# Sliding-window attention and an MLP mixer on one core: transpositions as units of their own, a planner with other constants, and new orders

## The chip, the cores and the metric

The kernel runs on one core of a Trainium2 chip. Five engines take part. TensorE (PE in the profile; PEld are its weight loads) multiplies matrices into PSUM, VectorE (DVE), ScalarE (ACT) and GpSimd (POOL) read PSUM or SBUF and write SBUF, and SyncE (SP) only issues DMAs. GpSimd issues DMAs too: all loads that change the type from float32 to bfloat16 go through its queue. The metric is the device time of one execution in microseconds (us). Three executions of the kernel before took 195.54, 192.81 and 198.23 us, so its median is 195.54 us.

## The reference

Four batches, eight heads, 768 positions, 64 channels a head. A query sees the last 128 positions and the first four (the sinks). The mixer follows, over positions (w_tok1, w_tok2) and then over channels (w_ch1, w_ch2).

```python
scores = scale * np.matmul(q, k.transpose(0, 1, 3, 2))
keep = is_sink | in_window                    # first 4 keys, or the last 128
scores = np.where(keep, scores, -1000000000.0)
a = np.exp(scores - np.max(scores, axis=-1, keepdims=True))
a = a / (np.sum(a, axis=-1, keepdims=True) + 1e-09)
x = np.matmul(a, v)                           # then heads side by side: (4, 768, 512)
...
xt = x.transpose(0, 2, 1)
h = np.maximum(xt @ w_tok1, 0.0) @ w_tok2
u = x + h.transpose(0, 2, 1)
h2 = np.maximum(u @ w_ch1, 0.0) @ w_ch2
return (u + h2).astype(np.float32)
```

## The kernel before, in words

Attention goes by 16 **pairs**: pair p holds two heads of batch p // 4. Pairs 0 to 3 load q and k as float32 on SyncE's queue and cast them on an engine; pairs 4 to 15 load them as bfloat16 on GpSimd's queue (`load_q_or_k`, L1398), one DMA each for pairs 4 to 7 and two halves each from pair 8 on. v goes to six buffers on GpSimd's queue (`load_v`, L177; pair p uses buffer p % 6), with a column of ones that sums the softmax's denominators.

q and k have to stand with the channels on the partitions. For pairs 0 to 7 TensorE transposes them into PSUM (`turn`, L586, or `transposed`, L604), and ScalarE or VectorE copies them to SBUF (`prepare`, L514). From pair 8 on (`BY_DMA`) SyncE issues DMA transposes from SBUF to SBUF (L542). There are three buffers for the transposed k (`kTb`, L214: kT0, kT1, kT2; pair p uses kT of p % 3). After the transposition the sinks' columns of kT are copied to a tile kTs (L196, by GpSimd or VectorE, and by ScalarE for the early pairs).

Then come, for each pair: scores in three groups (`scores`, L640), for pairs 0 to 3 with the mask added by a matmul ahead of them (`masked`), an exp on ScalarE into pT (L680), for later pairs a mask applied to pT by VectorE (L699) or GpSimd (L691), the sinks' scores for two pairs at a time (`score_sinks`, L718), and pT times v (`pv`, L745), whose result VectorE divides by the sum of the weights (L766, L769) into x_sb.

The mixer over positions is `mix_h` (L870, with w_tok1) and `mix_u` (L902, with w_tok2). Its result u is transposed by TensorE in the first batches and by DMA in the later ones (L931). The mixer over channels is `mix_channels`: a first stage with w_ch1 (`v1`, or seven products of sums in place of eight products in `by_seven`, L1108, with the differences of L1094) and a second stage with w_ch2 that always goes by seven products of sums (`products`, L1250; the sums of w_ch2 are made by L1471, those of v1 by L1216; VectorE adds the products up in o_sb, L1262; SyncE or ScalarE stores o_sb, L1272).

**What sets the order.** TensorE's work is cut into units, in named streams: s scores, m masks, t transpositions and o pT times v of pairs 0 to 3; g and h the mixer over positions of batch 0; a the scores of pairs 4 to 15, called bursts, two groups each (`burst`, L469); v pT times v and k the mixer over positions of the later pairs and batches; c the first stage over channels; x and y the second stage (x of two row tiles, y of one). The string `ORDERED` says in which order units are issued on TensorE: "k4 y0 a9" is unit 4 of stream k, unit 0 of y, unit 9 of a. The string `LOADS` is the order of GpSimd's loads after the first ones: q5, k5 and v5 belong to pair 5, t1 and t2 are the two w_tok, c0 to c3 the parts of w_ch1, d0 to d3 those of w_ch2. Everything else (which engine copies what, when, which PSUM bank a unit gets, where on each queue a DMA stands) is chosen while the program is built, by a planner (`Plan`, from L320): it keeps a clock for each engine with assumed costs and issues whatever can begin first by that clock (`other`, L383; `commit_pe`, L405; `run`, L425). A load is taken to be finished `RECEIPT` ns after the queue's assumed time, and no more than `LANES` loads may be under way. On the chip each engine then runs its instructions strictly in the order written, with waits on semaphores.

In the kernel before, the transpositions of q and k of pair p + 1, for pairs 5 to 7, are a piece (`transposed`) of the burst that holds the first scores of pair p. So bursts a2, a3 and a5 start with 48 small transposing matmuls (units a0 and a1 are pair 4's transpositions).

## Time and profile before

| | |
|---|---|
| median of three executions | 195.54 us (192.81 to 198.23) |
| the profiled execution | 194.1 us, span of its instructions 192.1 us |
| TensorE busy | 180.8 us (94%), 2270 matmuls recorded of 2273 |
| VectorE, ScalarE, GpSimd busy | 161.1, 109.1, 81.9 us |
| granted TensorE clock | 1.00 |
| software DMA queue (GpSimd's loads) | 11.80 MB, 56864 packets |
| hardware DMA queue (SyncE's and ScalarE's) | 13.64 MB, 25136 packets |

The 2.0 us between the span and the execution's own time are around the program: before its first and after its last instruction. TensorE is the engine with the most work. An idle stretch of TensorE before the last matmul lengthens the run unless a later wait becomes shorter by it; idle time elsewhere counts only if TensorE comes to wait for it.

### The profile page before, as it was taken

How to read it: one execution, taken by the hardware profiler on the slowest of the kernel's cores; microseconds unless marked ns; L12 is line 12 of the kernel's file. 1: busy time of each engine (PE TensorE's matmuls, PEld its weight loads, DVE VectorE, ACT ScalarE, POOL GpSimd, SP SyncE). 2: the span in 40 equal slices, each digit the busy share in tenths (PEclk: the TensorE clock that was granted, in tenths of full speed). 3: DMA queues.
4: the chain of work that ended last, by engine and by line, in shares of the span. 5: the costliest groups of instructions: out<-in, count | busy, mean ns of one | idle time of the engine just before them, and what ended most of it. 6: DMA issues, size and time to landing. Idle time of an engine off the chain costs nothing.

```text
span 192.1 us, 5590 instructions
## 1 busy us (share of the span) xinstructions
PE 180.8 (94%) x2270; PEld 132.9 (69%) x2273; DVE 161.1 (84%) x340; ACT 109.1 (57%) x205; POOL 81.9 (43%) x132
## 2 busy tenths in 40 slices
PE   6688979799999999999999999999999999999992
PEld 1345667467667778885776789876777887667881
DVE  4466667697999799999999999989999986699953
ACT  4698858998896551528955760767453111773000
POOL 7198856497865398994262493040000000000000
PEclk9999999999999999999999999999999999999999
DMA  5999999999999999999999996250211204400144
GB/s 177 252 309 193 187 197 194 178 179 173 152 167 151 122 116 144 167 143 281 158 147 125 151 116 136 109 218 3 58 29 27 55 3 164 164 3 0 55 138 139
DMA packets 82601, 26.32 MB, mean 137 GB/s; under 512 B 70032, under 2 KB 80272, under 8 KB 82576
## 3 DMA queue, kind: packets, MB, share of 16 engines
q0 software_dynamic: 56864, 11.80, 77.6%
q1 hardware_dynamic: 25136, 13.64, 36.3%
q10 hardware_dynamic: 576, 0.52, 0.8%
q8 instruction: 18, 0.29, 0.6%
q14 instruction: 7, 0.06, 0.1%
HBM read 26.75 MB, written 6.29 MB: 172 GB/s over the span
## 4 chain that ended last, share of the span: by engine, by line
PE 60%; DMA 30%; DVE 3%; POOL 2%; issue 2%; SPq 0%
PE ps L187 60%; DMA w_ch<-in_moe_w_ch_dram 19%; DMA q_f<-in_q_dram 7%; DMA w_tok<-in_moe_w_tok_dram 4%; DVE q_f L1471 1%; DVE v_sums L1216 1%; POOL k_bf L172 1%; DVE o_sb L1262 1%; POOL v_aug L180 1%; DVE pT L699 1%; POOL w_ch L205 1%; SPq L135 0%; POOL q_bf L196 0%; PE ps L584 0%
## 5 line engine op out<-in xcount | busy, mean ns | idle before, releaser
L680 ACT ACTIVATE pT<-ps 128x1024 bf16<-128x1024 f32 (+1 forms) x48 | 44.0, 956 | 13.7 <-PE ps L187 13.6
L194 ACT ACTIVATE parts<-ps 128x384 f32<-128x384 f32 x54 | 24.4, 493 | 26.7 <-PE ps L187 22.5
L187 PE MATMUL ps<-uT,w_ch 128*128 128x384 bf16 x168 | 34.0, 326 | 0.1
L187 PEld LDWEIGHTS <-v1T 128*128 128x128 bf16 x288 | 27.8, 98 | 5.9 <-DVE q_f L1471 0.5
L1150 DVE CUSTOM_DVE_ANT_0 v1T<-ps,parts 128x384 bf16<-128x384 f32 x54 | 28.6, 552 | 3.4 <-PE ps L187 2.5
L187 PEld LDWEIGHTS <-w_ch 128*128 128x128 bf16 x204 | 19.3, 98 | 11.0 <-issue 0.6
L200 ACT ACTIVATE v1T<-ps 128x384 bf16<-128x384 f32 x39 | 18.9, 495 | 8.6 <-PE ps L187 8.0
L187 PEld LDWEIGHTS <-v_sums 128*128 128x128 bf16 x216 | 20.8, 98 | 3.0 <-issue 0.6
L187 PE MATMUL ps<-uT_sums,k_f 128*128 128x384 bf16 x108 | 22.6, 326 | 0.0
L187 PEld LDWEIGHTS <-w_tok 128*128 128x128 bf16 x192 | 18.4, 98 | 4.4 <-issue 0.5
L691 POOL TENSOR_SCALAR_AFFINE_SELECT pT<-pT 128x256 bf16<-128x256 bf16 (+1 forms) x28 | 15.0, 569 | 13.4 <-issue 9.3
L180 POOL DMA_DIRECT2D v_aug<-in_v_dram x16 | 17.0, 1063 | 7.0 <-PE ps L187 3.6
L187 PE MATMUL ps<-q_f,v1T 128*128 128x256 bf16 x144 | 19.2, 273 | 0.3 <-DVE q_f L1471 0.2
L187 PEld LDWEIGHTS <-k_f 128*128 128x128 bf16 x144 | 13.7, 98 | 7.7
L187 PE MATMUL ps<-w_ch,v1T 128*128 128x256 bf16 x144 | 19.0, 273 | 0.0
L187 PE MATMUL ps<-v_aug,pT 128*128 128x65 bf16 x352 | 18.0, 194 | 1.0 <-DMA v_aug<-in_v_dram 1.0
L1262 DVE TENSOR_TENSOR o_sb<-ps,u_sb 128x512 f32<-128x512 f32 (+1 forms) x32 | 17.1, 548 | 1.9 <-PE ps L187 1.9
L187 PEld LDWEIGHTS <-pT 128*128 128x128 bf16 x352 | 16.1, 98 | 3.2 <-DMA v_aug<-in_v_dram 1.3
L187 PE MATMUL ps<-q_f,v_sums 128*128 128x256 bf16 x144 | 18.2, 273 | 0.2 <-DVE o_sb L1262 0.2
L769 DVE TENSOR_TENSOR x_sb<-ps,recip 128x384 bf16<-128x384 f32 x32 | 17.3, 552 | 0.6
L1262 DVE TENSOR_TENSOR o_sb<-ps,o_sb 128x256 f32<-128x256 f32 (+1 forms) x24 | 12.9, 551 | 3.4 <-PE ps L187 3.2
L172 POOL DMA_DIRECT2D k_bf<-in_k_dram x16 | 13.4, 840 | 5.0 <-DMA q_bf<-in_q_dram 2.7
(88 smaller groups left out, 293.3 us busy)
## 6 DMA issues: line engine op xcount, KB each, us to landing
v_aug<-in_v_dram POOLq DMA_DIRECT2D x16, 192.0 KB, 11.0
w_ch<-in_moe_w_ch_dram POOLq DMA_DIRECT2D x8, 384.0 KB, 10.0
out_dram<-o_sb SPq DMA_DIRECT2D x6, 512.0 KB, 2.8
out_dram<-o_sb SPq DMA_DIRECT2D x10, 256.0 KB, 2.8
q_f<-in_q_dram SPq DMA_DIRECT2D x4, 384.0 KB, 6.5
k_f<-in_k_dram SPq DMA_DIRECT2D x4, 384.0 KB, 6.8
q_bf<-in_q_dram POOLq DMA_DIRECT2D x16, 96.0 KB, 8.3
k_bf<-in_k_dram POOLq DMA_DIRECT2D x16, 96.0 KB, 10.7
```

What stands on the lines that cost most here:

```text
L172: in_order(nc.gpsimd.dma_start(out=out[:, h], in_=rows[:, h]))
L180: in_order(nc.gpsimd.dma_start(out=v_aug.rearrange("p i t d -> p (i t) d")[:, :, 0:D], in_=v[b].rearrange("h s d -> (h s) d")[2 * hp * S:2 ...
L187: issue(nc.tensor.matmul(*args, skip_group_check=True, **kwargs))
L194: in_order(nc.scalar.activation(out, in_, AF.Copy))
L200: in_order(nc.scalar.activation(out, in_, AF.Relu))
L205: return in_order(nc.gpsimd.dma_start(out=out, in_=in_))
L680: in_order(nc.scalar.activation(part(tiles["pT", p][:, :, ds(2 * g, 2)]), of_keys(tiles["ps_s", p, g])[:, :, 0:width(g)], AF.Exp, scale=scale,
L691: in_order(nc.gpsimd.affine_select(out=pt, in_=pt, compare_op=ALU.is_ge, fill=0.0, base=-n, pattern=[[0, nk], [1 - 2 * n, P]], channel_mul ...
L699: in_order(nc.vector.tensor_tensor(out=pt, in0=pt, in1=m, op=ALU.min))
L769: in_order(nc.vector.tensor_tensor(out=x_sb[b][:, ts(half, QH), ts(hp, 2 * D)].rearrange("p t (i d) -> p t i d", i=2), in0=tiles["ps_o", p ...
L1150: in_order(nc.vector._custom_dve(TENSOR_ADD_SAT, out=v1_of(i, half), in0=ps, in1=kept[:, n], s0=HUGE, s1=0.0,))
L1262: in_order(nc.vector.tensor_tensor(out=sb(*out), in0=tiles["ps_out", b, t0, key[0]], in1=in1(), op=ALU.add,))
```

## The change

Four edits, all of them in how the program is ordered; the arithmetic and the number of matmuls stay as they are.

1. The transpositions of q and k for pairs 5, 6 and 7 leave the bursts. Each becomes a unit of its own (one burst with the single piece `transposed`), in a new stream w: w0 and w1 are pair 4's q and k (a0 and a1 before), w2, w3 and w4 are pairs 5, 6 and 7. Stream a has 18 units in place of 20, all numbers two lower.
2. The planner takes a load to finish 600 ns later (`RECEIPT` 1500 to 2100) and allows seven loads under way where it allowed eight.
3. The planner lets two readers of one PSUM bank on different engines follow each other, the second 60 ns after the first has ended, where before it let them run side by side.
4. `ORDERED` and `LOADS` are new strings.

All lines below the string stand one line further down after the change, and those below the planner's class ten.

```diff
     ORDERED = (
-        "t0-1 m0-1 s0-1 t2 m2 s2 t3 m3 s3 o0 m4 s4 t4 m5 o1 s5 t5 o2 m6 s6 t6 m7 s7 t7 o3 m8 s8 o4 a0 s9-10 m9 "
...
+        "t0-1 m0 s0 m1 t2 s1 m2 t3 s2 m3 o0 s3 t4 m4 o1 s4 o2 t5 m5 s5 t6 m6 s6 w0 t7 m7 s7 m8 o3 s8 o4 s9 w1 "
...
     LOADS = (
-        "q4 v1 t1 k4 v2 t2 v3 k5 q5 k6 q6 c0 v4 c3 c2 v5 q7 v6 k7 q9 c1 k9 q8 d3 k8 d1 v7 v11 d0 k10 d2 v8 "
...
+        "q4 v1 k5 k4 t1 q5 v2 q6 t2 v3 k6 v4 v5 c1 d2 k7 q7 c2 q8 c3 c0 v6 v7 d0 k8 k9 d1 q9 k11 d3 k13 q11 "
+        "v8 q10 v9 v10 k10 q12 v11 k12 q13 q14 k14 k15 v12 q15 v13 v14 v15 "
     )
...
-    LATER = "cxyakv"
+    LATER = "cxyakvw"
...
-    LANES = 8
+    LANES = 7
...
-    RECEIPT = 1500.0
+    RECEIPT = 2100.0
...
+            self.reads = []
...
-                e = min(op.cost, key=lambda e: max(self.free[e], r) + op.cost[e] + BIAS * (e == "DVE"))
-                t = max(self.free[e], r)
+                at = {
+                    e: max([self.free[e], r] + [x[1] for x in op.reads if x[0] != e]) for e in op.cost
+                }
+                e = min(op.cost, key=lambda e: at[e] + op.cost[e] + BIAS * (e == "DVE"))
+                t = at[e]
...
+                    last = [None, 0.0]
+                    for r in readers:
+                        r.reads.append(last)
...
+                    for x in op.reads:
+                        x[:] = [o[2], self.free[o[2]] + 60.0]
...
         prepare(first)
-        units += [turn(first, n) for n in range(2)]
+        turned = [turn(first, n) for n in range(2)]
...
             if p + 1 < min(BY_DMA, last + 1):
-                with_first.append(transposed(p + 1))
+                turned.append(burst(transposed(p + 1)))
...
-        return units, tokens, out
+        return units, tokens, out, turned
...
-    streams.update(zip("akv", attention_and_tokens()))
+    streams.update(zip("akvw", attention_and_tokens()))
```

What the strings and the planner make of this is shown at three places.

GpSimd's instructions from the cast of v's sinks on, before: v_aug1, v_aug2 and v_aug3 are v of pairs 1 to 3, k_bf_287 is k of pair 4, the casts are q and k of pair 3.

```order
L196 CAST v_sink_143<-uT_sums_145 128x520
L180 DMA v_aug1_96<-in_v_dram 128x12x64
L205 DMA w_tok1_164<-in_moe_w_tok1_dram 128x6x256
L167 DMA k_bf_287<-in_k_dram 128x2x384
L180 DMA v_aug2_97<-in_v_dram 128x12x64
L196 CAST q_bf_345<-q_f_159 128x2x6x64
L205 DMA w_tok2_165<-in_moe_w_tok2_dram 128x2x768
L196 CAST k_bf_390<-k_f_161 128x2x6x64
L180 DMA v_aug3_98<-in_v_dram 128x12x64
```

The same place after the change: k_bf_272 and q_bf_325 are pair 5, k_bf_286 is pair 4, q_bf_436 is pair 6.

```order
L197 CAST v_sink_143<-uT_sums_145 128x520
L181 DMA v_aug1_96<-in_v_dram 128x12x64
L168 DMA k_bf_272<-in_k_dram 128x2x384
L168 DMA k_bf_286<-in_k_dram 128x2x384
L206 DMA w_tok1_164<-in_moe_w_tok1_dram 128x6x256
L168 DMA q_bf_325<-in_q_dram 128x2x384
L197 CAST q_bf_358<-q_f_159 128x2x6x64
L197 CAST k_bf_370<-k_f_161 128x2x6x64
L181 DMA v_aug2_97<-in_v_dram 128x12x64
L168 DMA q_bf_436<-in_q_dram 128x2x384
L206 DMA w_tok2_165<-in_moe_w_tok2_dram 128x2x768
L181 DMA v_aug3_98<-in_v_dram 128x12x64
```

v of pair 2 now stands behind both casts, w_tok2 behind three more loads of q and k, and w_tok2 is no longer between the two casts.

GpSimd's instructions around the loads of v of pair 8 (v_aug2_97) and of k of pair 10 (k_bf_1160), before. kT2 and kT0 are the transposed k of pairs 8 and 9; copying their sinks' columns waits for the DMA transposes.

```order
L172 DMA k_bf_1160<-in_k_dram 128x6x64 x2
L205 DMA w_ch2_167<-in_moe_w_ch2_dram 128x3x512
L180 DMA v_aug2_97<-in_v_dram 128x12x64
L691 AFFINE_SELECT pT_1127<-pT_1127 128x2x128 x2
L691 AFFINE_SELECT pT_1127<-pT_1127 128x128 x2
L172 DMA k_bf_1248<-in_k_dram 128x6x64 x2
L180 DMA v_aug4_99<-in_v_dram 128x12x64
L196 COPY kTs_142<-kT2_111 64x4 x2
L180 DMA v_aug3_98<-in_v_dram 128x12x64
```

The same place after the change: v of pair 8 is v_aug2_97 as before, k of pair 10 is k_bf_1560, k_bf_1348 is pair 13, q_bf_1381 pair 11 and q_bf_1456 pair 10.

```order
L206 DMA w_ch2_167<-in_moe_w_ch2_dram 128x3x512
L197 COPY kTs_142<-kT2_111 64x4 x2
L173 DMA k_bf_1348<-in_k_dram 128x6x64 x2
L173 DMA q_bf_1381<-in_q_dram 128x6x64 x2
L197 COPY kTs_142<-kT0_109 64x4 x2
L181 DMA v_aug2_97<-in_v_dram 128x12x64
L173 DMA q_bf_1456<-in_q_dram 128x6x64 x2
L701 AFFINE_SELECT pT_1445<-pT_1445 128x2x128 x4
L181 DMA v_aug3_98<-in_v_dram 128x12x64
L181 DMA v_aug4_99<-in_v_dram 128x12x64
L173 DMA k_bf_1560<-in_k_dram 128x6x64 x2
```

Both loads stood ahead of the two copies of the sinks' columns; now both stand behind them, k of pair 10 behind a masking of four instructions and two loads of v as well, and the last part of w_ch2 is issued ahead of them all.

VectorE's last instructions before, o_sb0 being the sums of two row tiles (unit stream x) and o_sb2 those of one (stream y):

```order
L1262 TENSOR_TENSOR o_sb0_3128<-ps_94,o_sb0_3128 128x2x256 x2
L1262 TENSOR_TENSOR o_sb2_3180<-ps_94,u_sb_2609 128x256
L1262 TENSOR_TENSOR o_sb2_3180<-ps_94,o_sb2_3180 128x256
L1262 TENSOR_TENSOR o_sb0_3128<-ps_94,u_sb_2609 128x2x256
L1262 TENSOR_TENSOR o_sb2_3180<-ps_94,u_sb_2609 128x256
L1262 TENSOR_TENSOR o_sb2_3180<-ps_94,o_sb2_3180 128x256
```

And after:

```order
L1272 TENSOR_TENSOR o_sb0_3129<-ps_94,o_sb0_3129 128x2x256
L1272 TENSOR_TENSOR o_sb2_3167<-ps_94,o_sb2_3167 128x256 x2
L1272 TENSOR_TENSOR o_sb0_3129<-ps_94,u_sb_2599 128x2x256
L1272 TENSOR_TENSOR o_sb2_3167<-ps_94,u_sb_2599 128x256
L1272 TENSOR_TENSOR o_sb0_3129<-ps_94,o_sb0_3129 128x2x256
```

The last sum of the program is now one of two row tiles (512 elements a partition, stored by SyncE) where it was one of one row tile (256 elements, stored by ScalarE).

1 line of the change is left out of this document (removed), and 25 rows, old and new, of the table ORDERED.

## The prediction

> **What bounds the kernel now.** I start with the busy times of the page and then the table of stages (busy microseconds in each stretch, then the granted clock, the DMA share and GB/s).
>
> ```profile
> PE 180.8 (94%) x2270; PEld 132.9 (69%) x2273; DVE 161.1 (84%) x340; ACT 109.1 (57%) x205; POOL 81.9 (43%) x132
> 0.00:8.00 8.00, 5.42 (x43) 2.00 (x43) 3.56 (x19) 4.22 (x7) 4.03 (x11) 1.00 0.81 207
> 8.00:16.00 8.00, 6.22 (x110) 3.50 (x114) 5.75 (x14) 7.24 (x14) 5.67 (x7) 1.00 1.44 278
> 16.00:24.00 8.00, 7.67 (x160) 5.00 (x162) 4.61 (x14) 7.06 (x12) 7.44 (x10) 1.00 1.67 187
> 24.00:40.00 16.00, 13.53 (x267) 9.89 (x267) 11.38 (x28) 13.11 (x27) 9.53 (x14) 1.00 1.67 188
> 40.00:72.00 32.00, 31.65 (x475) 22.96 (x464) 28.90 (x58) 23.92 (x46) 23.44 (x36) 1.00 1.93 150
> 72.00:128.00 56.00, 55.84 (x740) 43.35 (x738) 53.91 (x112) 31.45 (x54) 30.35 (x56) 1.00 1.56 154
> 128.00:184.00 56.00, 56.00 (x463) 42.42 (x461) 49.39 (x94) 22.08 (x49) 1.49 (x3) 1.00 0.20 59
> 184.00:192.00 8.00, 4.51 (x42) 3.79 (x39) 3.63 (x7) 0.00 (x0) 0.00 (x0) 1.00 0.47 154
> ```
>
> TensorE (the first busy figure) sets the time. It lacks 7.2 us of the first 40 (2.6 + 1.8 + 0.3 + 2.5), 0.5 us of the next 88 and nothing from 128 to 184 us; 3.5 us go behind its last matmul. So an order can win at most some 5 us, nearly all of it before 40 us. The same figures say what it can lose: from 40 us on no transfer is late now, and whatever becomes late there is paid in full.
>
> Next come TensorE's own rows in order of time; in brackets is its idle time and what ended it.
>
> ```profile
> 15.93 0.35 PE L158 MATMUL ps<-ident,q_bf 64*128 64x64 bf16 x12
> 26.08 0.36 PE L187 MATMUL ps<-v_aug,pT 128*128 128x65 bf16 x6 [1.00 <-DMA v_aug<-in_v_dram]
> 33.37 0.38 PE L187 MATMUL ps<-qT,kT 64*64 64x256 bf16 x8 [0.23 <-ACT pT L680]
> 35.46 0.40 PE L190 MATMUL ps<-ident,u_sb 128*128 128x128 bf16 x4 [0.84 <-ACT qT L194]
> 36.18 0.83 PE L190 MATMUL ps<-ident,u_sb 128*128 128x128 bf16 x12 [0.32 <-DVE u_sb L919]
> ...
> 67.51 0.83 PE L187 MATMUL ps<-q_f,v1T 128*128 128x256 bf16 x6 [0.22 <-DVE q_f L1471]
> 73.10 1.47 PE L187 MATMUL ps<-q_f,v_sums 128*128 128x256 bf16 x12 [0.16 <-DVE o_sb L1262]
> 75.50 0.35 PE L187 MATMUL ps<-v_aug,pT 128*128 128x65 bf16 x6
> 87.18 0.54 PE L187 MATMUL ps<-qT,kT 64*64 64x256 bf16 x16
> ```
>
> The last two have no bracket: v of pair 8 (75.50) and the transposed q and k of pair 10 (87.18) are there when TensorE comes.
>
> **The change, part by part.** The sum is made against the profiled execution, 194.1 us.
>
> *Switches of form.* TensorE's array changes between 128x128, 64x128, 64x64 and 64x32. Counted in the order, such changes go from 68 to 79: a transposition that left its burst needs its own switch, and so do score bursts now cut up by other units.
>
> ```profile
> 18.08 0.48 PE L187 MATMUL ps<-mask_add,ident 128*128 128x384 bf16 x2
> 18.50 0.34 PE L187 MATMUL ps<-qT,kT 64*128 64x256 bf16 x4
> ...
> 46.88 3.41 PE L187 MATMUL ps<-uT,w_ch 128*128 128x384 bf16 x20
> 50.13 1.04 PE L187 MATMUL ps<-h1T,w_tok 128*128 128x256 bf16 x8
> ```
>
> Without a switch 20 matmuls of 384 columns take 50.13 - 46.88 = 3.25 us, 0.163 each. The two at 18.08 take 0.42 to the next form: 0.42 - 0.33 = 0.09 us for a switch. Eleven are 1.0 us. Most of the new ones lie before 45 us, where TensorE waits anyway; that idle time is the cover. Ends 0 and 1.0; I take **+0.6**. The Trainium skill's TensorEngine Tiling (Array Packing), Key Properties, says that "Mode switching requires drain", a rule against this change. If a drain cost a matmul's whole duration beyond its share of the stream, 3.41 - 3.25 = 0.16 us by the row at 46.88, eleven would be 1.8 us and the time 1.2 us later; the row at 18.08 shows 0.09.
>
> *Pair 3's q.* Unit t6 (its transposition) now stands ahead of m6 and s6 and, counted, behind 145 matmuls instead of 151. GpSimd's cast ends no earlier than before:
>
> ```profile
> 15.06 0.81 POOL L196 CAST q_bf<-q_f 128x768 bf16<-128x768 f32 x1 [0.64 <-DMA q_f<-in_q_dram]
> ```
>
> It ends at 15.87, and TensorE starts at 15.93 without an idle stretch worth a bracket. Coming up to 0.8 us sooner it would wait that much; what is moved behind it then runs unchanged. Ends 0 and 0.8, **+0.4**.
>
> *Loads up to 30 us.* The two steps of the chain of waits that show loads give issue and time to landing:
>
> ```profile
> 15.83 7.38 DMA w_tok<-in_moe_w_tok_dram
> ...
> 50.01 16.86 DMA w_ch<-in_moe_w_ch_dram
> ```
>
> w_tok2 lands at 23.21. Now both casts come first (0.70 us sooner for the second cast, as w_tok2's issue is out from between), then v of pair 2 and q of pair 6, 1.04 and 0.72 us of issue. So w_tok2 is issued near 18.4 instead of 15.83, and with 7.4 to 8.7 us (the second end from the row below for v) it lands at 25.8 to 27.1. Its first use stands behind pair 2's pT times v, which began before 26.08, so it is wanted at about 25.5 to 26.5. v of pair 3, which costs 1.00 now, is issued near 19.3 and lands at about 28, but is used after four units with w_tok2.
>
> ```profile
> DMA to landing us min/median/max: 7.1/8.6/8.7
> ```
>
> (v, issued from 10 to 18 us.) One wait of 1.00 goes, one for w_tok2 of 0 to 1.6 comes, and one for v of pair 2, issued at 16.7 rather than 13.01, of 0 to 0.7. Ends -1.0 and +1.3; **+0.5**, as two waits replace one.
>
> *30 to 40 us.* The brackets at 33.37, 35.46 and 36.18 add up to 1.39 us: TensorE waits for copies of ScalarE, among them qT and kT of a pair whose transposition stood in the burst just before, and for the transposition of u. The new order puts pair 5's pT times v, a score burst and w4 between the transpositions of u. Ends -1.4 and 0; **-0.6**, less than half, because VectorE and ScalarE do the same copies (13.11 us busy of 16 on ScalarE).
>
> *w_ch2.* The last part of w_ch2 lands at 66.87 now and holds L1471's sums, which TensorE waits for at 67.51; the new list issues that part ahead of k13, q11 and v8. The brackets at 67.51 and 73.10 are 0.38 us. Ends -0.4 and 0; **-0.4**.
>
> *v of pair 8 and k of pair 10.* This is the dearest term. Both now stand behind the copies of the sinks' columns, which wait for DMA transposes (SyncE's row: issue; GpSimd's: copies).
>
> ```profile
> 54.45 3.42 SPq L542 DMA_TRANSPOSE kT<-k_bf  x1
> ...
> 66.42 0.42 POOL L196 COPY kTs<-kT 64x4 bf16<-64x4 bf16 x2 [0.19 <-DMA kT<-k_bf]
> 66.92 2.51 POOL L691 TENSOR_SCALAR_AFFINE_SELECT pT<-pT 128x256 bf16<-128x256 bf16 x4
> ```
>
> ```profile
> DMA to landing us min/median/max: 6.0/9.2/10.4
> ...
> DMA to landing us min/median/max: 14.6/15.1/15.6
> ...
> DMA to landing us min/median/max: 6.8/8.9/17.0
> ```
>
> These three are the transposes of k issued from 76 to 112 us, v from 57 to 61, and k from 69 to 92. In the new load list k of pair 9 follows two more large loads and fewer halves, so its transpose is issued at about the same time, 54. By the median of 9.2 the copy of kT0's columns would come at 63, by the row at 66.42. So v8 is issued at 63.5 to 66.8 and lands at 72 (8.6 us) to 82 (15.1 us). It is wanted at 75.50 less ten matmuls (it stands behind 1055, before 1065), 74.4. Ends 0 and 7.6; with fewer loads under way than at 57 us I stay near the first end: **+0.5**. Behind v8 come q10 (two issues of 0.8), the masks (2.51), v9 and v10 (about 1.0 each), then k10's two: its second issue is at 71 to 75, its landing 8.9 later at 80 to 84, the transpose 9.2 later at 89 to 93. Before, it was issued at 48 and had more than ten microseconds to spare. It is wanted at 87.18 plus twelve matmuls of 0.163 (1265 stand ahead, before 1253), so at 89.2, and half a microsecond later through v8. Ends 0 and 3.3 by these medians, 12 by the two longest landings; **+1.2**. No other work covers it: units are issued strictly in order, and all of c, x and y behind burst a9 wait.
>
> The Trainium skill's DMA: Bandwidth & Descriptors, Anatomy of one DMA, gives 2.0 us and the bytes at 436 GB/s for a software-queue load; as an estimate, 192 KB of v would take 2.5 us and this whole term would vanish, 1.7 us less. The trace disagrees: no row above is under 6 us.
>
> *The end.* The last sum is twice as wide and SyncE stores it.
>
> ```profile
> L1262 DVE TENSOR_TENSOR o_sb<-ps,o_sb 128x512 f32<-128x512 f32 x3 | 2.0, 688 | 1.2 <-PE ps L187 1.2
> L1262 DVE TENSOR_TENSOR o_sb<-ps,o_sb 128x256 f32<-128x256 f32 x4 | 1.7, 423 | 1.3 <-PE ps L187 1.3
> ...
> out_dram<-o_sb SPq DMA_DIRECT2D x10, 256.0 KB, 2.8
> ...
> out_dram<-o_sb ACTq DMA_DIRECT2D x4, 128.0 KB, 2.3
> ```
>
> 0.688 - 0.423 = 0.27 us for the sum and 0 to 0.5 for the store: **+0.5**, nothing runs beside it.
>
> The planner's constants act through the order alone. Which of ScalarE and VectorE copies what differs in places; VectorE has 2.1 us free from 72 to 128 us (53.91 of 56), so a copy more there is hidden as long as nothing waits for just that one. I count 0, with ends of -0.5 and +1.0.
>
> Sum: 0.6 + 0.4 + 0.5 - 0.6 - 0.4 + 1.7 + 0.5 = +2.7, so 196.8 us in an execution like the profiled one. That one was 1.4 us under the median of the three; I add half of it, since one more median may fall on either side: **197.5 us**.
>
> **The rivals.**
>
> *Late loads of pairs 8 and 10 (slower).* The place is GpSimd's queue at the copy of kT0's columns; it decides if that copy comes at 66.4, as now, and not at 63. v8 then lands at 75.4 or later (+1.0) and k10's transpose at 93 (+3.3 on 89.7, and 0.7 more for the longer landings of a queue filled at once): 5.0 instead of 1.7, so 200.1, with the half 200.8. For it: copy and latencies are rows of this trace. Against: SyncE has one transpose fewer ahead.
>
> *The waits before 40 us go (faster).* If the new units give every copy its time, the 1.00 at 26.08, the 1.39 up to 36.18 and 0.4 later go, the late loads are in time, and switches are hidden: 194.1 - 2.8 + 0.5 (end) = 191.8; with the switches' free end and no added half this stays about 191.5. Against: w_tok2 and v2 are issued 2.6 and 3.7 us later.
>
> *Nothing to see.* The transpositions were hidden in ScalarE's waits and the loads land as the fixed-cost rule has it: without the 1.7 and the 0.5 for early loads 194.6, with the half 195.3.
>
> **How the numbers follow.** Forecast 0.36 (of it 0.28 within 2% and 0.08 above, by the longer landings), late loads 0.32, nothing to see 0.18, faster 0.14. Two per cent is 3.9 us, about what a measurement of this kernel can tell from no change: 191.6 to 199.5 is "same". That gives faster 0.14, same 0.46, slower 0.40. The range leaves out half of the faster case and the longest landings: 192.5 to 202.5; the forecast's own is 195 to 200.
>
> **What would show it.** In the profile after: a TensorE bracket near 26 to 28 naming w_tok, none for v3 over 0.3; brackets at 33 to 37 below 1 us; brackets near 75 naming v_aug and near 89 naming kT or kTs, which together are 1 to 3 us, or about 5 in the slower rival; GpSimd's second copy of kTs at 63 or at 66; the last sum 0.69 us. I am wrong if 40 to 128 us lacks under 0.7 us of TensorE again, or if VectorE, not a DMA, ends the long waits there.

## The result and the profile after

The changed kernel takes **195.21 us** (median of 20 executions, 193.34 to 196.22). The kernel before takes 194.24 us (20 executions); the 195.54 from which the forecast started was the median of its first three. The ratio is **1.0058, with a 95% interval of 1.0032 to 1.0083**: about 1 us slower, within the 2 per cent that count as no change. Some executions of a kernel take over 1.5 per cent more than its fastest one; every ratio here is of the others alone, while the medians given in microseconds are of all. The profiled execution of the changed kernel took 194.8 us (span 193.1), that of before 194.1 (192.1).

First the table of stages of the changed kernel (columns as in the prediction: busy TensorE, weight loads, VectorE, ScalarE, GpSimd, then granted clock, DMA share, GB/s).

```profile
PE 183.6 (95%) x2273; PEld 133.6 (69%) x2273; DVE 160.1 (83%) x340; ACT 110.2 (57%) x203; POOL 80.6 (42%) x128
0.00:8.00 8.00, 5.73 (x38) 1.96 (x39) 3.46 (x18) 4.08 (x9) 4.02 (x11) 1.00 0.80 205
8.00:16.00 8.00, 7.74 (x121) 3.70 (x121) 5.01 (x15) 7.63 (x13) 5.77 (x8) 1.00 1.44 276
16.00:24.00 8.00, 8.00 (x182) 4.40 (x181) 5.83 (x16) 7.92 (x14) 7.88 (x10) 1.00 1.51 194
24.00:40.00 16.00, 14.96 (x337) 12.11 (x335) 12.13 (x33) 13.64 (x26) 9.03 (x14) 1.00 1.65 188
40.00:72.00 32.00, 30.68 (x366) 21.93 (x364) 28.16 (x56) 21.74 (x42) 18.18 (x28) 1.00 1.82 143
72.00:128.00 56.00, 55.43 (x734) 42.80 (x733) 51.90 (x106) 31.51 (x54) 33.43 (x57) 1.00 1.72 157
128.00:184.00 56.00, 56.00 (x462) 42.41 (x461) 50.35 (x96) 23.66 (x51) 2.27 (x4) 1.00 0.20 60
```

TensorE's idle time before 40 us has shrunk from 7.2 to 3.6 us, and yet the run is longer. From 40 to 184 us it has grown from 0.51 to 1.89 us. TensorE's own rows with a bracket from 24 us on (start, duration, then what, and in brackets the idle time ahead and what ended it; one of 0.17 at 96.27 is left out), and the same last group of matmuls in both kernels, say where:

```profile
25.32 0.19 PE L188 MATMUL ps<-v_aug,pT 128*128 128x65 bf16 x1 [0.53 <-issue]
28.20 0.36 PE L188 MATMUL ps<-v_aug,pT 128*128 128x65 bf16 x6 [0.16 <-DMA v_aug<-in_v_dram]
34.65 0.22 PE L188 MATMUL ps<-v_sink,pT_sink 128*128 128x130 bf16 x1 [0.33 <-DVE x_sb L779]
54.71 0.57 PE L594 MATMUL ps<-ident,u_sb 64*64 64x64 bf16 x48 [1.32 <-DVE u_sb L929]
89.18 0.55 PE L188 MATMUL ps<-qT,kT 64*64 64x256 bf16 x16 [0.39 <-DMA kT<-k_bf]
...
188.21 0.82 PE L188 MATMUL ps<-q_f,v1T 128*128 128x256 bf16 x6
189.06 0.69 DVE L1272 TENSOR_TENSOR o_sb<-ps,o_sb 128x512 f32<-128x512 f32 x1 [0.23 <-PE ps L188]
```

And of the kernel before:

```profile
187.69 0.82 PE L187 MATMUL ps<-q_f,v1T 128*128 128x256 bf16 x6
...
188.55 0.43 DVE L1262 TENSOR_TENSOR o_sb<-ps,o_sb 128x256 f32<-128x256 f32 x1 [0.23 <-PE ps L187]
```

The last matmuls start 0.52 us later. Since 1.38 us more of idle time came after 40 us, TensorE was some 0.9 us ahead there: that, and not 3.6, is what the change won early in these two executions. The other half microsecond of the span is the end.

The early 3.6 us mislead because the opening scatters from execution to execution. sums_behind_u, the first experiment below, has TensorE's order of the changed kernel:

```profile
8.00:16.00 8.00, 6.31 (x118) 3.50 (x120) 5.13 (x15) 7.71 (x14) 6.12 (x8) 1.00 1.40 273
...
7.16 0.60 PE L188 MATMUL ps<-mask_add,ident 128*128 128x512 bf16 x2
...
27.84 0.36 PE L188 MATMUL ps<-v_aug,pT 128*128 128x65 bf16 x6 [0.17 <-DMA v_aug<-in_v_dram]
```

It is busy 1.4 us less in that stretch and nevertheless reaches the matmuls at 28.20 in the profile above 0.36 us sooner. The reason for the difference in busy time is how long the same matmuls take. The two at 7.16 are in the changed kernel's profile

```profile
7.89 1.04 PE L188 MATMUL ps<-mask_add,ident 128*128 128x512 bf16 x2
```

and take 1.04 us where 0.60 is enough, although the column of the granted clock reads 1.00 in both. The kernel before, like sums_behind_u, takes 0.35 us for twelve transposing matmuls near 5.95, the changed kernel's profile 0.50; there the slow opening lasts to some 10 us. Its length differs from execution to execution. How long TensorE is counted busy there is no measure of how far it has come; the start of one and the same matmul is.

**The wait at 54.71** is the largest new one. VectorE's rows ahead of it, after and then (last two rows) before:

```profile
52.56 1.03 DVE L1481 TENSOR_TENSOR q_f<-w_ch 128x768 bf16<-128x768 bf16 x2 [2.76 <-DMA w_ch<-in_moe_w_ch_dram]
53.51 0.55 DVE L1481 TENSOR_TENSOR q_f<-w_ch,q_f 128x768 bf16<-128x768 bf16 x1
53.97 0.68 DVE L929 TENSOR_TENSOR u_sb<-ps,x_sb 128x512 bf16<-128x512 f32 x1
```

```profile
52.59 0.69 DVE L919 TENSOR_TENSOR u_sb<-ps,x_sb 128x512 bf16<-128x512 f32 x1 [0.40 <-PE ps L187]
53.20 1.15 DVE L1471 TENSOR_TENSOR q_f<-w_ch 128x768 bf16<-128x768 bf16 x2
```

Before, the last sum of u came first and the differences of w_ch2 behind it. Now the planner has put three differences ahead. VectorE stands still for 2.76 us until a part of w_ch2 lands, makes the differences, and only then the sum of u for which TensorE waits.

### The profile page after: what moved, and what is told of

The parts are those of the page before. It is cut to its first block, busy times and chain, and to the rows that moved or that the text cites. A ratio compares the mean times of both kernels' runs of the same rounds, so it can differ in the third digit from the quotient of the medians.

```text
span 193.1 us, 5587 instructions
## 1 busy us (share of the span) xinstructions
PE 183.6 (95%) x2273; PEld 133.6 (69%) x2273; DVE 160.1 (83%) x340; ACT 110.2 (57%) x203; POOL 80.6 (42%) x128
## 4 chain that ended last, share of the span: by engine, by line
PE 56%; DMA 27%; POOL 6%; DVE 4%; ACT 2%; issue 2%; SPq 0%; POOLq 0%; DVEq 0%; ACTq 0%
PE ps L188 55%; DMA kT<-k_bf 9%; DMA w_ch<-in_moe_w_ch_dram 8%; DMA v_aug<-in_v_dram 5%; DMA k_bf<-in_k_dram 4%; POOL v_aug L181 3%; DMA k_f<-in_k_dram 2%; ACT pT L690 1%; POOL pT L701 1%; DVE u_sb L929 1%; DVE pT L709 1%; POOL q_bf L173 1%; PE ps L159 1%; DVE q_f L1481 1%; ACT qT L195 0%
## 5 line engine op out<-in xcount | busy, mean ns | idle before, releaser
L1160 DVE CUSTOM_DVE_ANT_0 v1T<-ps,parts 128x384 bf16<-128x384 f32 x54 | 27.8, 550 | 2.8 <-PE ps L188 1.7
L188 PE MATMUL ps<-uT_sums,k_f 128*128 128x384 bf16 x108 | 23.8, 326 | 0.0
L188 PE MATMUL ps<-v_aug,pT 128*128 128x65 bf16 x352 | 18.5, 194 | 0.7 <-issue 0.5
L1272 DVE TENSOR_TENSOR o_sb<-ps,u_sb 128x256 f32<-128x256 f32 (+1 forms) x32 | 17.1, 550 | 2.4 <-PE ps L188 2.4
L188 PEld LDWEIGHTS <-pT 128*128 128x128 bf16 x352 | 16.9, 98 | 3.1 <-issue 0.9
L188 PE MATMUL ps<-q_f,v_sums 128*128 128x256 bf16 x144 | 18.8, 273 | 0.0
L188 PE MATMUL ps<-w_ch,v1T 128*128 128x256 bf16 x144 | 18.5, 273 | 0.0
L701 POOL TENSOR_SCALAR_AFFINE_SELECT pT<-pT 128x256 bf16<-128x256 bf16 (+1 forms) x20 | 12.6, 661 | 12.5 <-issue 10.0
L188 PE MATMUL ps<-qT,kT 64*64 64x192 bf16 (+2 forms) x336 | 14.7, 251 | 0.4 <-DMA kT<-k_bf 0.4
```

The lines of the kernel that those rows point to most:

```text
L188: issue(nc.tensor.matmul(*args, skip_group_check=True, **kwargs))
L701: in_order(nc.gpsimd.affine_select(out=pt, in_=pt, compare_op=ALU.is_ge, fill=0.0, base=-n, pattern=[[0, nk], [1 - 2 * n, P]], channel_mul ...
L1160: in_order(nc.vector._custom_dve(TENSOR_ADD_SAT, out=v1_of(i, half), in0=ps, in1=kept[:, n], s0=HUGE, s1=0.0,))
L1272: in_order(nc.vector.tensor_tensor(out=sb(*out), in0=tiles["ps_out", b, t0, key[0]], in1=in1(), op=ALU.add,))
```

## The experiments

Each ratio is to the kernel before in the same runs, with its 95% interval; the changed kernel's is 1.0058.

### Which of the new waits count

**sums_behind_u** puts the differences behind the sum of u again.

```diff
-            queue((name, c), Op({"DVE": 63.0 + 0.525 * k * DM // 2}, run, loaded + [done[n, c] for n in of]))
+            queue((name, c), Op({"DVE": 63.0 + 0.525 * k * DM // 2}, run, loaded + [("u", 1, 0, 4)] * (c == 0) + [done[n, c] for n in of]))
```

> The changed kernel with one change on VectorE alone: the first differences of w_ch2 (L1481) are issued behind the last sum of u for batch 1 (L929) and no longer ahead of it; every other engine has the same instructions in the same order. Both theories: the bracket of 1.32 us at 54.71 (TensorE waiting for VectorE's u_sb) shrinks to under 0.2. Theory A (a TensorE wait ahead of its last matmul is paid in full): 1.1 to 1.3 us faster than the changed kernel, 193.9 us by its median of 195.21, and the bracket at 89.18 (kT of pair 10) stays at 0.3 to 0.5. Theory B (the transposed k of pair 10 lands at a time that GpSimd's and SyncE's queues set, whatever TensorE does): the bracket near 88 to 89 grows from 0.39 to 1.4 to 1.7, and no more than 0.3 us is won, 194.9 to 195.2.

Measured: 195.40 us, 1.0073 (1.0033 to 1.0113). In the profile (span 192.2) TensorE's rows:

```profile
54.79 1.46 PE L188 MATMUL ps<-uT,w_ch 128*128 128x384 bf16 x8 [0.67 <-DVE x_sb L779]
...
88.30 0.54 PE L188 MATMUL ps<-qT,kT 64*64 64x256 bf16 x16 [0.60 <-DMA kT<-k_bf]
```

The 1.32 us are gone, 0.67 come back at the next instruction of VectorE that the differences hold up (x_sb), and the last matmuls start at 187.35, 0.86 us sooner. Of that, 0.36 us were there at 28 us already, long before the place of the edit, so some 0.5 are left for it. Pair 10's k landed 0.9 us sooner as well and the wait for it grew by 0.2 only, so theory B falls. Theory A has the bracket right and the time wrong: it asked for 1.1 to 1.3 us, and the interval of the ratio reaches only some 0.5 us below the changed kernel's 1.0058. So the wait and its cause are shown; that it costs the kernel the whole 1.3 us is not. The profiled execution, 193.93 us, is near the fast end of the twelve (193.31 to 198.0).

**k10_earlier** goes for the wait at 89.18.

```diff
-        "v8 q10 v9 v10 k10 q12 ..."
+        "v8 k10 q10 v9 v10 q12 ..."
```

> The changed kernel with one entry of the load list moved: k of pair 10 ahead of q of pair 10 and v of pairs 9 and 10 (the planner moves a few small copies of sinks with it). Its two halves are issued near 67.4 instead of 73.5, and the transpose lands near 82 to 84 instead of 89.1. Both theories: the bracket of 0.39 at 89.18 goes, and the one of 1.32 at 54.71 stays. Theory A: 0.4 us faster than the changed kernel, 194.8. Theory B: the same 0.4 us, if v of pairs 9 and 10 and q of pair 10, now 1.7 us later, are not waited for; if they are, a bracket naming v_aug or qT between 75 and 90 takes back as much, and the time stays at 195.2.

Measured: 196.53 us, 1.0143 (1.0095 to 1.0192), slower. The wait at 89 went, but at 74.7 came a new one:

```profile
73.38 0.82 DVE L197 COPY kTs<-kT 64x4 bf16<-64x4 bf16 x2 [0.72 <-DMA kT<-k_bf]
74.23 0.76 DVE L1272 TENSOR_TENSOR o_sb<-ps,o_sb 128x256 f32<-128x256 f32 x2
74.71 0.34 PE L188 MATMUL ps<-v_aug,pT 128*128 128x65 bf16 x6 [1.06 <-DVE o_sb L1272]
```

The planner had given copies of the sinks' columns to VectorE. There they wait for a DMA transpose, and sums that TensorE needs wait behind them: the mechanism of 54.71 at another place. A second such copy waits 1.74 us at 85.36, and TensorE 0.47 at 86.48. Neither theory had it.

**sums_and_k10** joins the two.

> The changed kernel with both: the differences of w_ch2 behind u, and k of pair 10 earlier. Theory A: the two gains add up, 1.3 + 0.4 = 1.7 us faster than the changed kernel, 193.5. Theory B: the same 1.7, but much more than the sum of the two alone (0.2 and 0.4), since only here nothing absolute stands behind the wait at 54.71. A third possibility: another late landing at 95 to 100 us (the bracket at 96.27 names VectorE's u_sb) takes back part; then brackets between 90 and 128 us exceed the 0.2 us of now.

Measured: 195.63 us, 1.0105 (1.0048 to 1.0162). The gains do not add up: the wait at 74.5 (1.0 for VectorE's o_sb) is there again, another of 1.0 comes at 120, and neither theory had these. The third possibility has a bracket beyond 90 us, though not at this place.

**k10_copies_on_gpsimd** is k10_earlier with these copies kept off VectorE, whose order is then the changed kernel's.

```diff
-                {"POOL": 700.0, "DVE": 370.0}, sinks_of, done["kT", p] + [("sk", p - NHP)],
+                {"POOL": 700.0}, sinks_of, done["kT", p] + [("sk", p - NHP)],
```

> As k10_earlier, but the sinks' columns of the transposed k may be copied by GpSimd only; VectorE then has exactly the instructions and the order of the changed kernel. In k10_earlier the planner had given two of these copies to VectorE, which stood still until a transpose had landed, and TensorE waited 1.1 us for VectorE at 74.7. Theory C (an instruction on VectorE that waits for a transfer holds up the ones behind it, and TensorE with them): the bracket near 74.7 is under 0.2, the one near 89 (kT of pair 10) is gone too, and the time is 0.4 to 0.5 us below the changed kernel's, 194.8. Rival (v of pair 8 itself is late because k of pair 10 is loaded at the same time): the bracket near 74.7 stays at 0.8 or more and names v_aug.

Measured: 194.11 us, **1.0001 (0.9967 to 1.0036)**. The row for v of pair 8, without a bracket:

```profile
73.05 0.35 PE L188 MATMUL ps<-v_aug,pT 128*128 128x65 bf16 x6
```

Theory C holds for the waits: with the same load list and TensorE's order unchanged, those at 74.7 and 86.5, 1.5 us together, are gone. The time is 1.4 per cent below k10_earlier's, 2.4 to 2.8 us, and 0.7 us better than the theory said, so not all of it comes from the copies. In this profile the wait at 54.71 is missing too, though VectorE has the changed kernel's order: the part of w_ch2 landed sooner (VectorE goes on at 51.42 us instead of 52.56), and 0.62 us for v1T come at 49.64 in its place. old_end and six_more_switches, further down, have VectorE's order of the changed kernel as well and show 1.31 and 0.33 us at that place. How long this wait is differs from execution to execution, and 1.32 is one of them.

**old_end** undoes the end alone.

```diff
-        "x50 x52-53 y25-26 x54-55 y27 x51"
+        "x50 x52-53 x51 y26 x54-55 y27 y25"
```

> The changed kernel with the end of the order as in the kernel before: the last product is one of one row tile, its sum 0.42 us instead of 0.69 and its store issued by ScalarE; all else is the same to the last 5 us. If the end costs what the two profiles show (4.07 us behind the last matmul's start instead of 3.56): 0.5 us faster than the changed kernel, 194.7. If the stores of the other tiles end last anyway: no change, 195.2.

Measured: 195.32 us, 1.0090 (1.0054 to 1.0126): no gain that the scatter would let through. The last sum is 0.42 us instead of 0.69, as it was before, so 0.27 of the term is sure. The rest is what lies behind the last sum, and that scatters: from the start of the last six matmuls to the end of the span it is 5.2 us here (193.5 - 188.34) with the narrow sum, 4.9 in the changed kernel and 5.6 in k10_copies_on_gpsimd, both with the wide one.

**four_repairs**: sums_behind_u, k10_copies_on_gpsimd, old_end, and the part of w_ch2 for the first differences earlier.

```diff
-        "... c0 v6 v7 d0 k8 k9 ..."
+        "... c0 d0 v6 v7 k8 k9 ..."
```

> The changed kernel with four repairs: the first differences of w_ch2 behind u on VectorE; the second part of w_ch2 for them (d0) loaded ahead of v of pairs 6 and 7; k of pair 10 loaded earlier with the copies of sinks on GpSimd; the end of the order as before. Theory C: the bracket of 1.32 at 54.71 goes, and the 0.67 that replaced half of it in sums_behind_u (x_sb at 54.79) stays under 0.3, since VectorE no longer stands still for w_ch2; the 0.4 to 0.7 at 89 goes; the last sum is 0.27 shorter. Together 1.9 to 2.3 us below the changed kernel, about 193.1, and 0.5 to 1.0 below the kernel before. Theory A' (what is won at one place is lost at the next late landing): v of pair 6 or 7, issued 0.8 us later, or v of pairs 9 and 10 is waited for, 0.5 us or more, and no more than 0.8 us is won: 194.4 or more.

> four_repairs once more, unchanged. Expected: 193.0 to 193.7 us and a ratio of 0.992 to 0.998 to the kernel before in the same runs; with the first 12 executions an interval that leaves out 1.

Measured: 193.47 us, **0.9953 (0.9924 to 0.9982)**, and again 193.92 us, **0.9991 (0.9960 to 1.0021)**. All of TensorE's brackets from 40 to 128 us in the first of these:

```profile
51.88 0.81 PE L188 MATMUL ps<-uT,w_ch 128*128 128x384 bf16 x4 [0.24 <-ACT v1T L201]
94.40 0.22 PE L188 MATMUL ps<-v_sink,pT_sink 128*128 128x130 bf16 x1 [0.17 <-DVE u_sb L929]
```

Against the changed kernel this is faster both times (1.0058 against 0.9953 and 0.9991, the intervals do not touch). Against the kernel before one interval leaves out 1 and the other does not, so a lead over it is not shown. One repair alone, k10_copies_on_gpsimd, has an interval (0.9967 to 1.0036) that overlaps both, so what the other three add is not shown either.

**five_repairs** issues w_tok2 ahead of q of pair 6 as well ("v2 t2 q6" for "v2 q6 t2").

> four_repairs with w_tok2 issued ahead of q of pair 6 instead of behind it, 0.7 us sooner. In four_repairs TensorE waits 0.3 us (0.5 by the starts of its matmuls) for w_tok2 at 26.6. Theory A (a late w_tok2 costs what the forecast said, in full): the bracket goes, 0.3 to 0.5 us faster than four_repairs, 193.0. Rival (it was hidden by v of pair 3, which lands at 28.2 in any case): the bracket near 28 naming v_aug grows by as much, and the time stays at 193.5.

Measured: 196.13 us, 1.0106 (1.0044 to 1.0169). The rival has the bracket: w_tok2 is in time, but v of pair 3 is waited for 0.50 us instead of 0.16. The time is 2.7 us worse than the rival's 193.5. The profile, of the fastest of the six executions (194.43 us), shows one reason: the planner, with other landings, again let a sum of u come late.

```profile
27.15 0.36 PE L188 MATMUL ps<-v_aug,pT 128*128 128x65 bf16 x6 [0.50 <-DMA v_aug<-in_v_dram]
...
51.31 2.11 PE L188 MATMUL ps<-uT,w_ch 128*128 128x384 bf16 x12 [1.05 <-DVE u_sb L929]
```

### The price of a switch

**six_more_switches** reorders TensorE inside six bursts.

```diff
-    def burst(*pieces):
+    def burst(*pieces, between=False):
...
+        turns = list(pieces)
+        if between and turns[-1].form == EIGHTHS:
+            turns.insert(len(turns) - 2, turns.pop())
+
         def run():
-            for p in pieces:
+            for p in turns:
                 p.fn()
...
-            units.append(burst(*pieces))
+            units.append(burst(*pieces, between=True))
```

> The changed kernel with TensorE's order altered inside six bursts only: the four matmuls of the sinks' scores (64x32) stand between the two scores' groups (64x64) and no longer behind both, so that the array changes its form 85 times in place of 79; all other engines and all other matmuls are in the same order. By the forecast's price, 0.09 us for a switch, 0.5 us in all; if a change away from a narrow form waits until the running matmuls have drained (0.12 to 0.32 us from the last start in a narrow form to the next in another form, in both profiles), 0.17 us each and 1.0 in all. In the profile: from the first matmul of each of the six bursts to the first one behind it 0.09 or 0.17 us longer. The time: 195.7 or 196.2, a small difference beside the scatter, so the bursts decide.

The last of the six bursts in the changed kernel, and in this one:

```profile
123.73 0.52 PE L188 MATMUL ps<-qT,kT 64*64 64x192 bf16 x16
124.18 0.40 PE L188 MATMUL ps<-qT,kTs 64*32 64x512 bf16 x4
124.51 0.83 PE L188 MATMUL ps<-w_ch,v_sums 128*128 128x256 bf16 x6
```

```profile
124.53 0.33 PE L188 MATMUL ps<-qT,kT 64*64 64x192 bf16 x8
124.78 0.40 PE L188 MATMUL ps<-qT,kTs 64*32 64x512 bf16 x4
125.11 0.38 PE L188 MATMUL ps<-qT,kT 64*64 64x256 bf16 x8
125.42 0.83 PE L188 MATMUL ps<-w_ch,v_sums 128*128 128x256 bf16 x6
```

From the first matmul of the burst to the first one behind it: 0.78 before (124.51 - 123.73), 0.89 now (125.42 - 124.53). By the starts of the single matmuls it is 0.777 and 0.894 us, the same to a few ns in all six: **0.117 us for a switch**, between the forecast's 0.09 and its other price of 0.16. If the eleven of the change, most of them between other forms, cost the same, they are 1.3 us: an estimate. Time: 195.34 us, 1.0067 (1.0034 to 1.0099), too close to 1.0058 to tell.

### The parts of the change alone

**readers_side_by_side** takes the rule on two readers of a bank away.

```diff
-                at = {
-                    e: max([self.free[e], r] + [x[1] for x in op.reads if x[0] != e]) for e in op.cost
-                }
+                at = {e: max(self.free[e], r) for e in op.cost}
```

> The changed kernel with one of the planner's three rules as before: two readers of one bank may run side by side. Seven loads and the later landings stay. VectorE's order differs in some 20 places, GpSimd's in one. If the 3.9 per cent of old_planner_rules came from this rule: 2 to 8 us slower than the changed kernel, with a bracket of over 2 us near 70. If it came from the assumed landings, which set where VectorE's long sums stand: within 0.8 us of the changed kernel's 195.2.

Measured: 195.60 us, 1.0073 (1.0031 to 1.0115), as the changed kernel, so the 3.9 per cent of old_planner_rules, which comes next, are not from this rule alone. In the profile there are waits of 1.16 for ScalarE's kT at 34.7 (0.33 before) and 0.90 for its v1T at 48.5, and none at 54.7.

**old_planner_rules** takes all three rules away (that, and `LANES = 8`, `RECEIPT = 1500.0`).

> The changed kernel with the planner's three rules as before: a load is taken to have landed 600 ns sooner, eight loads may be under way, two readers of one bank may run side by side. Orders and units stay the changed ones. My forecast counted the rules at nothing, from -0.5 to +1.0 us. Theory A: where VectorE and ScalarE do their copies changes at many places, so the brackets before 60 us differ, but their sum stays within 1.0 us of the changed kernel's, and the time within 0.8 us of it. Rival (the rules are needed with these orders): VectorE's differences of w_ch2, planned sooner, hold it up more, the bracket near 54 us grows above 1.8 us or others of over 1 us appear, and the time is 1.5 us or more above the changed kernel's.

Measured: 203.83 us, **1.0387 (1.0308 to 1.0466)**; the rival holds. In the profile TensorE waits 1.73 us for ScalarE's pT at 32.95, 1.37 for its v1T at 50.26, and 1.16 and 3.11 for VectorE's x_sb at 63.87 and 73.30. With the reader rule alone at 1.0073, the number of loads under way and the assumed landing are what is left, alone or together with it; they were not tried apart.

**two_units_back** returns two of the three transpositions to their bursts.

```diff
-        "m9 s10-11 m10 w2 g0 s12 g1 o5-6 a0 g2-3 o7 a1 o8 ... v0 w3 h1 ..."
+        "m9 s10-11 m10 g0 s12 g1 o5-6 w2 a0 g2-3 o7 w3 a1 o8 ... v0 h1 ..."
```

> The changed kernel with the transpositions of pairs 5 and 6 put back right ahead of the bursts with the first scores of pairs 4 and 5 (the place they had in the kernel before); pair 7's stays apart, since the planner finds no order with all three. Four switches of the array's form fewer (75 for 79). Theory A (the units apart hide ScalarE's and VectorE's copies of qT and kT): brackets of 0.7 to 1.4 us in all that name qT or kT come back between 26 and 38 us, less 0.5 us for the four switches: 0.2 to 0.9 us slower than the changed kernel. Rival (the copies were hidden anyway, the switches are what the change costs): no such bracket over 0.3, and 0.3 to 0.6 us faster.

Measured: 202.10 us, **1.0390 (1.0327 to 1.0453)**. TensorE's larger brackets, and the table of stages around the largest:

```profile
28.74 0.38 PE L163 MATMUL ps<-ident,q_bf 64*64 64x64 bf16 x22 [0.71 <-ACT u_sb L195]
30.14 0.38 PE L188 MATMUL ps<-qT,kT 64*64 64x256 bf16 x8 [0.72 <-ACT pT L690]
32.33 0.22 PE L188 MATMUL ps<-v_sink,pT_sink 128*128 128x130 bf16 x1 [1.20 <-issue]
...
70.86 1.94 PE L188 MATMUL ps<-x_sb,w_tok 128*128 128x256 bf16 x9 [2.36 <-DVE x_sb L779]
```

```profile
68.00:70.00 2.00, 0.51 (x5) 0.30 (x4) 2.00 (x4) 0.05 (x1) 2.00 (x3) 1.00 1.71 109
70.00:72.00 2.00, 1.14 (x7) 0.82 (x7) 1.41 (x3) 0.00 (x0) 1.95 (x4) 0.76 1.85 151
72.00:74.00 2.00, 1.72 (x20) 0.78 (x19) 0.00 (x0) 1.12 (x4) 2.00 (x5) 0.50 2.03 162
```

Neither theory holds. Theory A has the sign, and 2.6 us of waits come back from 28 to 33 us, but none of them names qT or kT, and the longest, 1.20, has no releaser in the profile. Most of the 7 us is something else: TensorE waits 1.33 us for ScalarE's v1T at 49.87; VectorE is busy all through 68 to 70 us with sums of v1 and o_sb that stand ahead of x_sb, and TensorE waits 2.36 us for it; and in the two rows behind that the granted clock is 0.76 and 0.50.

**units_apart** does the reverse: before's orders, loads and planner, only the transpositions as units ("a0 s9-10 m9 g0-1 m10 a1 s11-12" becomes "w0 s9-10 m9 g0-1 m10 w1 s11 w2 s12", w3 stands behind h1, w4 right behind a1).

> The kernel before with the transpositions of pairs 5 to 7 as units of their own, each 3 to 5 units ahead of the burst it was part of; loads, planner and the order of all other units as before (73 switches for 68, 0.6 us at 0.12). Theory A (the units apart hide ScalarE's copies): the brackets at 33 to 36 us shrink from 1.39 to under 0.7, and the time is the kernel before's within 0.6 us. Theory D (the order of units, the loads and the planner only work together; a part alone lets VectorE's queue fall into another order): brackets of over 1 us naming VectorE come between 40 and 75 us, and the time is 1.5 to 4 per cent longer, as in two_units_back and old_planner_rules.

Measured: 200.55 us, **1.0364 (1.0319 to 1.0410)**. The largest bracket is one that neither theory has:

```profile
27.11 0.38 PE L163 MATMUL ps<-ident,q_bf 64*64 64x64 bf16 x24 [3.46 <-DMA q_bf<-in_q_dram]
```

w2 now comes before its q has been loaded. The new load list has q5 and k5 at places 6 and 3, the old one at 9 and 8: in the changed kernel these loads stand earlier, as its earlier units need them. Theory D has the time and not the mechanism: no bracket of over 1 us names VectorE from 40 to 75 us (the longest, 0.77, is at 42.76); besides the 3.46 there are 1.15 us for a load of k at 40.69.

**before_d2_earlier** tries the repair of w_ch2 on the kernel before, which also waits for VectorE's differences (at 67.51).

```diff
-        "... d0 k10 d2 v8 ..."
+        "... d0 d2 k10 v8 ..."
```

> The kernel before with one entry of its load list moved: the last part of w_ch2 (d2) ahead of k of pair 10. In the kernel before VectorE stands 1.4 us for it at 66.9 and TensorE then for VectorE, at 67.5 and in short waits up to 73 (0.38 us in brackets, 1.1 in all by the starts of its matmuls). If one late part of w_ch2 costs the kernel before what another costs the changed one: VectorE's wait under 0.3, no TensorE bracket from 66 to 74, and 0.7 to 1.1 us faster, 193.3 to 193.7, as fast as the changed kernel with its repairs; the change would then be worth nothing beside where w_ch2 lands. If k of pair 10, now 0.8 us later, or the short waits stay: within 0.3 us of the kernel before.

Measured: 201.13 us, 1.0381 (1.0330 to 1.0432). VectorE no longer waits for w_ch2, but the planner gave it a copy that waits 1.5 us for a transpose (at 61.54), and TensorE waits 5.9 us in three brackets for x_sb, 3.1 of them at 68.8. So once more, with the copies on GpSimd:

> The kernel before with d2 (the last part of w_ch2) ahead of k of pair 10, and the copies of sinks' columns of the transposed k allowed on GpSimd only. Theory C (an instruction on VectorE that waits for a transfer is what costs): without the copies on VectorE the wait of 3.1 us for x_sb near 69 of before_d2_earlier goes and with it most of the 3.8 per cent; VectorE's wait for w_ch at 66.9 is gone as well: 193.3 to 194.4. Rival (VectorE's long sums, now planned sooner, stand ahead of x_sb and hold up TensorE whether VectorE waits or not): a bracket naming x_sb of over 1.5 us between 66 and 72 stays, and the time is 197 or more.

Measured: 198.75 us, 1.0234 (1.0189 to 1.0279). The rival holds:

```profile
67.08 0.75 DVE L1216 TENSOR_TENSOR v_sums<-v1T,v_sums 128x1152 bf16<-128x1152 bf16 x1
67.75 0.55 DVE L769 TENSOR_TENSOR x_sb<-ps,recip 128x384 bf16<-128x384 f32 x1
68.35 2.08 PE L187 MATMUL ps<-x_sb,w_tok 128*128 128x256 bf16 x9 [4.15 <-DVE x_sb L769]
```

VectorE waits for no transfer here and is still too late: theory C was too narrow. What costs is what stands ahead on VectorE, whether it waits or works. The two runs differ by 1.5 of the 3.8 per cent; since keeping the copies off VectorE moved other instructions too, that is not the price of the copies alone. Whether the kernel before could gain from an earlier d2 with VectorE's order kept stays open.

## Why the prediction was right or wrong

The direction and the class (within 2 per cent) were right, and 195.21 lies in the range of 192.5 to 202.5. The point, 197.5, was 2.3 us too high, the result at the very edge of the forecast's own range (195 to 200). Of the +2.7 us only +0.7 came (between the profiled executions). The step that failed is the dearest term, the landings of v of pair 8 and k of pair 10: +1.7 forecast, 0.39 measured; they were taken too long. That the direction came out right is in part luck: the largest wait that makes the changed kernel the slower one, 1.32 us at 54.71 for VectorE, is in no term of the sum, and k10_copies_on_gpsimd, whose profile has neither it nor the 0.39, is level with the kernel before (1.0001). The terms:

- **The starting point.** Half of the 1.4 us between the three-run median and the profiled execution was added. The median of 20 is 194.24, and the step was 0.6 us too large: the profiled execution was the better estimate.
- **v of pair 8 and k of pair 10, +1.7.** The place was right and the landings were wrong. The copy of kT0's columns on GpSimd did come nearly as late as the slower rival feared, but the loads behind it landed much sooner than assumed:

```profile
65.75 0.73 POOL L197 COPY kTs<-kT 64x4 bf16<-64x4 bf16 x2 [0.31 <-DMA kT<-k_bf]
...
DMA to landing us min/median/max: 5.0/5.6/8.5
...
DMA to landing us min/median/max: 5.6/6.3/7.0
```

  The last two are v issued from 60 to 80 us and k of pair 10. The forecast took 8.6 to 15.1 and 8.9 from rows of stretches in which, counted by the issues and landings of GpSimd's loads, four to seven others were under way. Here GpSimd had stood 5.29 us, up to 61.55, waiting for pair 8's transpose, and had issued nothing; when v of pair 8 was issued, at 66.43, four were under way, and three at k of pair 10. v of pair 8 landed after 5.5 us and was not waited for. The second half of k of pair 10 was issued at 74.33, inside the forecast's 71 to 75, landed 7.0 us later and its transpose another 7.7 (8.9 and 9.2 forecast): 3.4 us sooner, and the wait 0.39 in place of up to 3.3 (0.6 to 0.9 in the experiments that leave it where it is). The slower rival fell with its landings, not with its place.
- **w_ch2, -0.4.** Its two brackets (67.51, 73.10) went, as forecast. But the step looked only at the last part and TensorE's brackets; that the differences of the first half would move ahead of the sum of u on VectorE was not looked at, and TensorE waited 1.32 us for it at 54.71. The forecast had named VectorE, not a DMA, ending the long wait there as a sign of being wrong; so it was, with a DMA behind VectorE.
- **The planner's constants, 0.** Wrong in kind: they do act through the order alone, but VectorE's order is where the new wait came from, and with the old rules the same orders take 3.9 per cent longer.
- **30 to 40 us, -0.6, and loads up to 30 us, +0.5.** Better than forecast. The brackets from 24 to 40 us went from 2.39 (1.00, 0.23, 0.84, 0.32) to 1.02 (0.53, 0.16, 0.33). w_tok2 landed at 26.6, inside the 25.8 to 27.1 forecast, and was only just waited for (0.30 in four_repairs, 0.53 in sums_and_k10, no bracket in the changed kernel's profile).
- **Pair 3's q, +0.4.** Nothing in the changed kernel's profile: the cast started sooner (14.61) and had ended when TensorE came, at 15.48. But TensorE came late there, through its slow opening. In sums_behind_u (third row), with the same cast at the same time, it was early and waited 0.47, and in four more profiles 0.16 to 0.30. The term was right in place and about right in size; it is hidden in this one execution.

```profile
14.61 0.82 POOL L197 CAST q_bf<-q_f 128x768 bf16<-128x768 f32 x1 [0.59 <-DMA q_f<-in_q_dram]
...
15.48 0.40 PE L159 MATMUL ps<-ident,q_bf 64*128 64x64 bf16 x12
...
15.49 0.35 PE L159 MATMUL ps<-ident,q_bf 64*128 64x64 bf16 x12 [0.47 <-POOL q_bf L197]
```

- **Switches, +0.6.** The price was low: 0.117 us in the one kind of switch that was added alone, by which eleven would be 1.3 us where the upper end was 1.0. How much of it was hidden can't be separated.
- **The end, +0.5.** From the last matmul's start on, 0.5 us longer in the two profiles, 0.27 of it the wider sum; the rest is within what old_end shows of the scatter there.

So the sum of +2.7 us was +0.7 between the profiled executions and +1.0 between the medians. The time is that of the rival "nothing to see" (195.3), but not by its reason: in the two profiles 0.9 us are won before 40 us, 1.4 lost after, 0.5 at the end. The faster rival had the place right (the brackets before 40 us did shrink, by 1.4) and the size wrong: by the last matmuls they were worth 0.9. Which part of the change won these could not be separated, since no part ran alone without a new wait.

## What to carry to other kernels

When a planner decides the order, compare the order on every engine that the busiest one waits for, and look at what now stands ahead of each instruction that it waits for: three small differences, or a copy of four columns, ahead of a needed sum made longer waits here (1.32 and 1.06 us) than the loads of the forecast's dearest term (0.39). Take a transfer's landing time from a stretch in which as many others are under way as there will be. Orders, load list and planner's rules that were found together could hardly be priced one at a time: five attempts to take or move one made the one or the other kernel 2.3 to 3.9 per cent slower, mostly by waits at places that the part itself doesn't touch. The exceptions are a rule that made no difference (readers_side_by_side) and a load moved with VectorE's order held (k10_copies_on_gpsimd).

## What was not expected of the hardware

- **Some idle stretches of TensorE were paid for again.** Single waits of up to 1.4 us left the granted clock at 1.00. After the 2.36 us of two_units_back the rows above show it at 0.76 and 0.50, and the next two microseconds at 0.89; after the 3.46 of units_apart it fell too (0.50 from 28 to 30 us, 0.66 from 30 to 32), and after only 1.73 in old_planner_rules (0.56 and 0.58 in the two stretches from 34 to 38 us). Each time these figures add up to some 3.4 us at half the clock; by them, an estimate, up to 1.7 us are lost on top of the wait. The Trainium skill's TensorE: Matmul & The Clock Gate, What's actually happening, states that an idle window of about 3.4 us halves the clock and that the window runs freely; the trace agrees on the half, and shows it after brackets of 1.73 and 2.36 us already.
- **The price of a switch of form.** One more change, from 64x32 back to 64x64, cost 0.117 us in each of six bursts, to a few ns. The Trainium skill's TensorEngine Tiling (Array Packing), Key Properties, has the rule that a change of mode drains TensorE, without a figure; the 0.117 us of the trace are less than the duration of one matmul (251 ns is the mean of the qT,kT ones in the changed kernel's profile).
- **A load's landing follows how many are under way.** The same 192 KB of v landed 5.0 to 5.7 us after its issue with three or four other loads under way in the changed kernel (pairs 8 to 10), and 14.6 to 15.6 us after it with seven in the kernel before.
